# Loads of the late units in a fused attention and feed-forward kernel: start, place and planned slack

## The chip, the cores and the metric

The kernel runs on one core of one Trainium2 chip. The metric is device time in microseconds (us) of one execution; three timed runs of the kernel before stand beside one profiled execution. TensorE does the matrix products, VectorE (DVE), ScalarE (ACT) and GpSimd (POOL) the elementwise work, SyncE (SP) issues most transfers and GpSimd the others.

## The reference

Cosine attention over 8 batches, 12 heads, 448 positions and 64 columns, then a feed-forward layer with a cosine gate over all 3584 rows:

```
q_n = q / (norm(q) + 1e-6);  k_n = k / (norm(k) + 1e-6)
attn = exp(q_n @ k_n.T / tau - max);  attn = attn / (sum + 1e-9)
x = (attn @ v), heads side by side        # 3584 x 768
h = x @ w_in                              # 768 x 2048
out = (h * cos(h)) @ w_out                # 2048 x 768
```

Inputs and outputs are float32; the products are made in bfloat16.

## The kernel before

**Units and pairs.** The 96 heads are cut into 16 *units* of 6 heads (`u` from 0 to 15, two units for each batch), and each unit into 3 *pairs* of heads (`g` from 0 to 47). A pair takes four score products (`scores`, L709 and L717) with an exponential behind each (ACT, L724), and the attention products of the pair before (`attend`, `split`: L746 and L738 for most pairs). Sums of the exponentials of a unit are counted by matmuls (`counts`, L770), inverted, written to DRAM and read back spread over the partitions (`chain`: gather L907, spread L902 or L915, broadcast L917 into `RB`), and GpSimd makes the normalised `xT` (L922).

**First and second product.** When both units of a batch are done, `m1` makes the first product of that batch, `x @ w_in` (L935): 16 tiles in 8 steps of two, each step followed by a cosine on ScalarE (L964) and a multiplication on VectorE (L966) that gives `gT` of that step. The second product (`m2_fill`, `m2_quarters`: L1034, L1063) is cut into small pieces and filled in between the products of the following pairs. `points` names the pairs after which a first product comes: pair 12 for batch 1, and 21, 27, 33, 39, 45 for batches 2 to 6.

**The way of a unit's inputs.** `load` brings q and k of one pair of heads into `raw` (L582, two transfers on SP's queue); `raw` has two buffers, for even and odd units. GpSimd squares them (`square`, L622), VectorE sums (L629), ScalarE or GpSimd makes the inverse root, GpSimd scales (L660, `qks`), and a transfer on SP's queue transposes into `qkT` (L677, a ring of three). So the loads of unit u+2 can begin when the scaling of unit u is done. `load_v` brings a unit's v into `va` (L596, two issues on GpSimd's queue; three buffers).

**The planner.** All this is written down as a list of operations with what they read and write. `Program.arrange` plays the list through with a cost for each operation: TensorE's operations keep nearly their order (it may take one of the next eight), while on the other engines, SP's and GpSimd's queues included, each time one of the operations that are ready is taken, the one that is due first, due times being counted back from TensorE's. The outcome is the fixed order of each engine; on the chip semaphores hold the data's order. Three things steer it here. `behind` puts a transfer behind another one in its queue, without a wait for that one's data. `reads` adds a real dependency. `pad` (2.5 us, `LATE`, for loads of unit 2 and later) makes the planner expect a load's data later than it computes, and changes no instruction of its own.

**Where the late loads stand.** In `pair`, at the first pair of an even unit u, the loads of unit u+2 are put behind the broadcast of unit u-1 (`bcast`); at the last pair of an even unit, the loads of unit u+3 behind the same broadcast. At the first pair of each unit `load_v` of a later unit is put behind a making of `xT` ("x%d"), with exceptions in `PLAN["vloads"]`. From pair `behind0` on, if pair g-1 is normalised by the chain (not "direct"), the first attention product of pair g-1 is listed behind the first score product of pair g and a filling of the second product; before that pair it is listed ahead of both.

Of the kernel before, what the change touches and what calls it, by code (L numbers as in the profile page):

```python
# [13 lines left out]
PLAN = {  # L14
    "apart": 1,
    "ahead": (1, 2),
    "halves": tuple(range(25)),
    "folded": (0, 1, 2, 3),
    "grid": {2: (16, 5, 6), 3: (11, 3, 4), 4: (8, 2, 3)},
    "hold": 0.6,  # L20
    "margin": 1.0,
    "sq": ["AA", "A", "A", "P", "P", "P"],
# [4 lines left out]
    "late4": {1: (7, "T9"), 2: (8, "T10")},  # L27
    "power": (2,),
    "late": 0.0,
    "behind0": 13,  # L30
    "inverted": (5, 7, 9, 11, 13, 15),
    "bi": 0.0,
    "sooner": {8: 20, 12: 20},
# [20 lines left out]
    "given": {13:(0,0,2,3),16: (4, 0, 5, 2), 22:(1,2,5,6), 26:(3,2,5,6), 27:(0,0,3,2), 34: (12, 4, 5, 6), 46: (12, 4, 3, 4), 47: (4, 0, 5, 0)},  # L54
    "roots": (3, (8, 0), (10, 0), (12, 0), (14, 0)),
    "lead": {33: 5, 45: 5, 12: 13, 21: 13},
    "vloads": {3: [(4, "x6"), (5, "x6")], 4: [(6, "x11")], 5: [], 6: [(7, "x15"), (8, "x15")]},
    "behind": {2: 8, 3: 0, 4: 8},
    "direct": (0, 1, 2, 3, 4, 5, 7, 8, 9, 10, 11, 17, 23, 47),
}  # L60
# [340 lines left out]
def bass_cosine_attention__then__act_gcu_kernel(  # L401
# [30 lines left out]
    LATE = 2.5  # L432
# [22 lines left out]
    gT = sb("gT", [128, NF * RING], BF16)  # L455
# [123 lines left out]
    def load(u, p0, p1, apart=False, eng="SP", behind=None, reads=()):  # L579
        i = u % 2  # L580
        h = slice(2 * p0, 2 * p1)
        f = [lambda e, x=x, t=t: e.dma_start(  # L582
            rawv[i][BP * x : BP * x + BP, h].rearrange("p h s d -> p h (s d)"), src(t, u, 2 * p0, 2 * (p1 - p0)))
            for x, t in enumerate((k, q))]
        for x in ((0,), (1,)) if apart else ((0, 1),):
            behind = P.ops[-1] if x == (1,) else behind
            dma(eng, [f[y] for y in x], list(reads), [("raw", i, p, y) for p in range(p0, p1) for y in x] + (["first"] if (u, p0) == (0, 0) and 1 in x else []),
                "raw%d_%d_%s" % (i, p0, x), 0.97 * (p1 - p0) * len(x), "load u%d p%d" % (u, p0), behind, 1.8,
                pad=LATE if u > 1 else 0.0)

    def load_v(u, behind=None, reads=()):
        if u >= NU:
# [349 lines left out]
    def m1(b, early=0, split=NKC, turn=TURN, order=tuple(range(NKC)), done=0, inner={}):  # L942
        table(SINSET)

        def names(gi):
            return BANKS.get(PHs[turn[gi]][0], [PHs[turn[gi]][0]])

        def step(gi, a, c0, c1):
            m1_step(b, turn[gi], 2 * gi + a, c0, c1, order)

        for gi in range(done):
            for a in range(2):
                step(gi, a, NKC - 2, NKC - 1)
        for c0, c1 in [(0, split)] + [(c, c + 1) for c in range(split, NKC - 1)]:
            for gi in range(done, early):
                for a in range(2):
                    step(gi, a, c0, c1)
        for gi in range(NF // 2):
            for g in inner.get(gi, ()):
                transposes(g)  # L960
            ph, cz = PHs[turn[gi]][1], gi % 2
            for a in range(2):
                step(gi, a, NKC - 1 if gi < early else 0, NKC)
            act(lambda e, ph=ph, cz=cz: e.activation(cosv[cz], ph[:, :, 0:S], ACT.Sin, bias=cst.ap()[:, 0:1], scale=1.0),  # L964
                names(gi) + ["cst0"], [("cos", cz)], 2 * S, "S", 1, label="sin%d.%d" % (b, gi))
            dve(lambda e, ph=ph, cz=cz, gi=gi: e.tensor_tensor(  # L966
                gTv[:, 2 * gi : 2 * gi + 2, S * (b % 2) : S * (b % 2) + S], ph[:, :, 0:S], cosv[cz], ALU.mult),
                names(gi) + [("cos", cz)], [("gT", b % 2, gi)], 2 * S, label="g%d.%d" % (b, gi))
        table(EXPSET)
# [13 lines left out]
    def m2_add(b):  # L983
        for t in range((b * S) // 128, ((b + 1) * S) // 128):
            w = [0, HW, DM]
            if t == B * S // 128 - 1 and PLAN["tail"]:
                w.insert(2, HW + PLAN["tail"])
            for hf, x in enumerate(zip(w, w[1:])):
                m2_queue.append([t, hf, 0, None, x])
# [108 lines left out]
    def find(label):  # L1098
        return [o for o in P.ops if o.label == label][-1]
# [23 lines left out]
    def direct(g):  # L1123
        return g in PLAN["direct"]
# [16 lines left out]
    points = {PB * (b + 1) + (PLAN["second"] if b == 1 else 3): b for b in range(1, B - 1)}  # L1141

    def pair(g, f):
        u, p = g // UP, g % UP
        if 3 <= u < NU - 1:
            if p == 0:
                norms(u + 1, 0)
            if p == u % 2:
                norms(u + 1, 1)
        late = g > PB  # L1150
        quarters = g >= PB
        if late and not direct(g - 1):
            f = (f[0] + f[1], 0) + f[2:]
        behind = g - 1 in points or g >= PLAN["behind0"] and not direct(g - 1)
        if late and not behind and g - 1 not in PLAN["quarters"]:
            attend(g - 1, direct(g - 1), (0,))
        scores(g, 0)
        m2_fill(f[0], quarters)
        if late and behind and g - 1 not in PLAN["quarters"]:
            attend(g - 1, direct(g - 1), (0,))  # L1160
        scores(g, 1)
        if late and g - 1 in PLAN["quarters"]:
            m2_fill(f[1], quarters)
            attend(g - 1, direct(g - 1), (3, 0))
            scores(g, 2)
            attend(g - 1, direct(g - 1), (1, 2))
        elif late and direct(g - 1):
            attend(g - 1, True, (1, 2))
        elif late:
            attend(g - 1, False, (1,))  # L1170
            m2_fill(f[1], quarters)
            if not f[1]:
                scores(g, 2)
            attend(g - 1, False, (2,))
        elif 1 <= g < PB:
            if g in PLAN["ahead"] and g + 1 < PB:
                transposes(g + 1)
            attend(g - 1, direct(g - 1))
        closes = g > PB and not direct(g - 1) and (g % UP == 0 or direct(g))
        closes = closes and g not in points  # L1180
        if closes:
            if f[1]:
                scores(g, 2)
            m2_fill(f[2], quarters)
            counts((g - 1) // UP)
        if g >= 1 and g != PB:
            if closes:
                chain((g - 1) // UP)
            if g % UP == 0:
                if g > PB and (u <= 3 or u % 2 == 0):  # L1190
                    for x in range(UP if u + 2 < NU else 0):
                        load(u + 2, x, x + 1, behind=find("bcast%d" % (2 if u == 4 else u - 1)) if u > 3 else
                             find(PLAN["u5"][x]) if u == 3 else None)
                if g > PB:
                    for x, y in PLAN["vloads"].get(u, [(u + 2, "x%d" % (g - 1 if u % 2 == 0 else g - 4))]):
                        load_v(x, find(y))
        if g == PB:
            m2_fill(f[1], True)
        if g + 2 < PB:
            norms((g + 2) // UP, (g + 2) % UP)  # L1200
        if g + 1 < PB and g not in PLAN["ahead"]:
            transposes(g + 1, g + 1 < PLAN["apart"])
        if max(TD, PB + 2) <= g + 2 < NG and g + 2 >= LT:
            transposes(g + 2)
        for x, (y, t) in PLAN["late4"].items():
            if y == g:
                load(4, x, x + 1, behind=find(t))
        if PLAN["v3"] and g == PLAN["v3"][0]:
            load_v(3, None, [PLAN["v3"][1]])
        if not closes:  # L1210
            if not late or direct(g - 1) and g - 1 not in PLAN["quarters"] or not direct(g - 1) and f[1]:
                scores(g, 2)
            m2_fill(f[2], quarters)
        scores(g, 3)
        m2_fill(f[3], quarters)
        if p == UP - 1 and u >= 3 and u % 2 == 0:
            loads(u + 3, find("bcast%d" % (u - 1)) if u > 4 else None)
# [37 lines left out]
    for g in range(PB, NG):  # L1255
        pair(g, PLAN["six"] if g == PB else PLAN["given"][g] if g in PLAN["given"] else shares(PLAN["cycle"].get(g, 2)))
        if g in points:
            if 0 < m2_at() and m2_at() + 6 >= 2 * NF:
                m2_fill(2 * NF - m2_at(), True)
            if not direct(g - 1):  # L1260
                counts((g - 1) // UP)
                chain((g - 1) // UP)
            if points[g] == 1:
                m1(1, 2, *PLAN["mixed"])
            else:
                m1(points[g], 2, UP, PLAN["turns"].get(points[g], AFTER))
            m2_add(points[g])
            m = (NF - 5 - m2_at()) % NF or NF
            m2_fill(PLAN["lead"][g] if g in PLAN["lead"] else m + NF if m < 8 else m, True)
# [50 lines left out]
```

## Time and profile before

| | us |
|---|---|
| median of 3 runs | 422.16 |
| lowest, highest | 420.97, 422.93 |
| the profiled execution, its own time | 421.63 |
| its span, first to last instruction | 419.8 |
| TensorE busy | 408.0 |
| ScalarE busy | 272.6 |
| GpSimd busy | 248.3 |
| VectorE busy | 198.2 |
| mean granted TensorE clock | 0.996 of full speed |

All times of the profile are counted from the first instruction of the span. "Busy" of TensorE is the time in which at least one matmul is in the array; matmuls are pipelined, and their ends are modelled. PEld are its weight loads, which overlap. "SPq" and "POOLq" are the issues of transfers. In a row of the timeline the bracket gives the idle time before the instructions and what ended it; "issue" means that the profile shows nothing that the engine waited for. In a row of the waits the three numbers are the total in us, the number of times and the longest. A row of the stretches has the stretch, its length, busy time and instructions of PE, PEld, DVE, ACT and POOL, the granted clock, the DMA share and GB/s. DMA queue q8 carries instructions: packets, MB and share.

### The profile page before, as it was taken

How to read it: one execution, taken by the hardware profiler on the slowest of the kernel's cores; microseconds unless marked ns; L12 is line 12 of the kernel's file. 1: busy time of each engine (PE TensorE's matmuls, PEld its weight loads, DVE VectorE, ACT ScalarE, POOL GpSimd, SP SyncE). 2: the span in 40 equal slices, each digit the busy share in tenths (PEclk: the TensorE clock that was granted, in tenths of full speed). 3: DMA queues.
4: the chain of work that ended last, by engine and by line, in shares of the span. 5: the costliest groups of instructions: out<-in, count | busy, mean ns of one | idle time of the engine just before them, and what ended most of it. 6: DMA issues, size and time to landing. Idle time of an engine off the chain costs nothing.

```text
span 419.8 us, 13928 instructions
## 1 busy us (share of the span) xinstructions
PE 408.0 (97%) x6213; PEld 245.6 (59%) x6213; DVE 198.2 (47%) x277; ACT 272.6 (65%) x386; POOL 248.3 (59%) x196
## 2 busy tenths in 40 slices
PE   7899999999999999999999999997999999999997
PEld 3354556755666656664567556773567655655555
DVE  4474753446753277245833376332853344313511
ACT  5897588894989557894588547881488735714500
POOL 4999985889493796878392994639664311020000
PEclk9999999999999999999999999998999999999999
DMA  8999999989878996499838994799914920141023
GB/s 189 251 251 226 207 211 211 234 128 224 124 108 171 211 278 117 104 219 184 194 71 152 199 232 111 110 204 191 218 28 86 187 69 3 44 116 38 2 66 85
DMA packets 78736, 63.54 MB, mean 151 GB/s; under 512 B 41844, under 2 KB 72916, under 8 KB 78676
## 3 DMA queue, kind: packets, MB, share of 16 engines
q1 hardware_dynamic: 60468, 49.96, 56.2%
q0 software_dynamic: 18048, 12.59, 20.8%
q8 instruction: 49, 0.80, 0.9%
q10 hardware_dynamic: 160, 0.10, 0.1%
q14 instruction: 11, 0.09, 0.1%
HBM read 54.98 MB, written 11.19 MB: 158 GB/s over the span
## 4 chain that ended last, share of the span: by engine, by line
PE 90%; DMA 3%; ACT 3%; DVE 2%; issue 1%; POOL 0%; SPq 0%; ACTq 0%
PE MP L1034 27%; PE SC L935 20%; PE AV L935 12%; PE SC L709 6%; PE AV L746 4%; PE MP L1063 4%; PE AV L770 4%; PE SC L1063 3%; DMA va<-in_v_dram 3%; PE MP L935 2%; PE AV L819 2%; ACT PX L724 1%; PE AV L810 1%; PE AV L803 1%; PE SC L717 1%
## 5 line engine op out<-in xcount | busy, mean ns | idle before, releaser
L724 ACT ACTIVATE PX<-SC 128x448 bf16<-128x448 f32 (+1 forms) x192 | 149.1, 825 | 14.8 <-PE SC L709 8.8
L1034 PE MATMUL MP<-W,gT 64*64 64x384 bf16 x2816 | 135.6, 323 | 0.7 <-DVE qkT L698 0.6
L1034 PEld LDWEIGHTS MP<-W,gT 64*64 64x64 bf16 x2816 | 81.0, 107 | 34.8 <-issue 4.8
L660 POOL TENSOR_TENSOR qks<-raw,rn 128x896 bf16<-128x896 f32 (+1 forms) x48 | 79.6, 1678 | 21.9 <-ACT rn L652 21.5
L935 PE MATMUL SC<-xT,W 128*128 128x448 bf16 x444 | 91.5, 354 | 0.0
L622 POOL TENSOR_TENSOR sq<-raw 128x896 bf16<-128x896 f32 x44 | 73.5, 1688 | 8.5 <-DMA raw<-in_q_dram 7.3
L922 POOL TENSOR_TENSOR xT<-xu,RB 128x448 bf16<-128x448 f32 x34 | 37.8, 1137 | 55.4 <-DMA RB<-scr 55.4
L935 PEld LDWEIGHTS SC<-xT,W 128*128 128x128 bf16 x444 | 43.3, 98 | 40.7 <-issue 1.3
L964 ACT ACTIVATE cosb<-SC,cst 128x896 f32<-128x896 f32 x37 | 37.3, 1007 | 38.7 <-PE SC L935 36.8
L935 PE MATMUL AV<-xT,W 128*128 128x448 bf16 x276 | 60.9, 357 | 0.7 <-issue 0.7
L629 DVE TENSOR_REDUCE n<-sq 128x14 f32<-128x896 bf16 (+2 forms) x49 | 51.6, 1058 | 5.7 <-ACT sq L620 4.7
L966 DVE TENSOR_TENSOR gT<-SC,cosb 128x896 bf16<-128x896 f32 x37 | 40.2, 1088 | 26.8 <-ACT cosb L964 26.7
L709 PE MATMUL SC<-qkT 64*64 64x448 bf16 x576 | 52.4, 353 | 0.3
L964 ACT ACTIVATE cosb<-AV,cst 128x896 f32<-128x896 f32 x23 | 23.2, 1008 | 40.7 <-PE AV L935 39.1
L756 DVE COPY xu<-AV 128x448 f32<-128x448 f32 x34 | 21.2, 625 | 51.5 <-PE AV L738 51.5
L935 PEld LDWEIGHTS AV<-xT,W 128*128 128x128 bf16 x276 | 26.9, 99 | 26.0 <-DVE xs L781 1.1
L1001 DVE COPY osb<-MP 128x384 f32<-128x384 f32 x26 | 14.5, 557 | 47.7 <-PE MP L1034 36.6
L746 PE MATMUL AV<-PX,va 64*64 64x448 bf16 x408 | 35.6, 349 | 0.0
L966 DVE TENSOR_TENSOR gT<-AV,cosb 128x896 bf16<-128x896 f32 x23 | 25.0, 1088 | 21.3 <-ACT cosb L964 21.3
L889 POOL TENSOR_TENSOR xT<-xu,RB 128x448 bf16<-128x448 f32 x8 | 9.1, 1135 | 29.9 <-ACT RB L885 29.9
L596 POOL DMA_DIRECT2D va<-in_v_dram x32 | 22.1, 694 | 7.0 <-DMA raw<-in_q_dram 4.2
L709 PEld LDWEIGHTS SC<-qkT 64*64 64x64 bf16 x576 | 17.3, 106 | 12.4 <-ACT PX L724 5.6
(84 smaller groups left out, 390.5 us busy)
## 6 DMA issues: line engine op xcount, KB each, us to landing
raw<-in_k_dram SPq DMA_DIRECT2D x48, 224.0 KB, 5.6
raw<-in_q_dram SPq DMA_DIRECT2D x48, 224.0 KB, 6.1
out_dram<-osb SPq DMA_DIRECT2D x54, 192.0 KB, 3.5
va<-in_v_dram POOLq DMA_DIRECT2D x32, 192.0 KB, 8.3
RB<-scr SPq DMA_DIRECT2D x18, 336.0 KB, 4.5
W<-in_moe_w_in_dram POOLq DMA_DIRECT2D x4, 768.0 KB, 14.7
W<-in_moe_w_out_dram POOLq DMA_DIRECT2D x4, 768.0 KB, 19.2
RB<-scr SPq DMA_DIRECT2D x6, 224.0 KB, 3.7
```

The lines of the kernel that those rows point to most:

```text
L622: pool(lambda e, x=x, y=y: e.tensor_tensor(y, x, x, ALU.mult), src_, dst, 0.1 + n * 1.78e-3, label="sq%d.%d" % (u, p)).pad = LATE if u > 1 ...
L629: dve(lambda e, w=w: e.tensor_reduce(out=n2v[i][:, 2 * p : 2 * p + 2, w], in_=sqv[p][:, :, w, :], axis=mybir.AxisListType.X, op=ALU.add), ...
L660: f = lambda e, s0=s0, s1=s1: e.tensor_tensor(qksv[i][:, p, s0:s1].rearrange("p s h d -> p h s d"), rawv[i][:, h, s0:s1, :], bass.AP(rn[i] ...
L709: m = e.matmul(SCv[z][BP * o : BP * o + BP, a, 0:S], t[r, c - 1 + (NT3 + 1) * o, 0:BP], t[r, :, BP : 2 * BP], start=True, stop=True)
L724: act(lambda e: e.activation(PHv[j] if c == 0 else PXv[j][:, c - 1], SCv[z][:, :, 0:n], ACT.Exp, scale=1.0 / TAU), ["SC%d" % z], [("PX", j ...
L746: m = e.matmul(AVv[64 * a : 64 * a + 64, o, 0:S], vav[y][r, 2 * p + a, c + 1, :], PXv[j][r, c, a, :], start=(c == 0), stop=False)
L922: f = lambda e, p=p: e.tensor_tensor(xTv[b % 2][:, UP * i + p, :].rearrange("p (s o m) -> p o s m", s=NB, o=2), xuv[:, u % 3, p, :].rearra ...
L935: t = e.matmul(ph[:, a, 0:S], W1v[:, order[c], 128 * n : 128 * n + 128], xTv[b % 2][:, order[c], :], start=(c == 0), stop=(c == NKC - 1))
L964: act(lambda e, ph=ph, cz=cz: e.activation(cosv[cz], ph[:, :, 0:S], ACT.Sin, bias=cst.ap()[:, 0:1], scale=1.0), names(gi) + ["cst0"], [("c ...
L966: dve(lambda e, ph=ph, cz=cz, gi=gi: e.tensor_tensor(gTv[:, 2 * gi : 2 * gi + 2, S * (b % 2) : S * (b % 2) + S], ph[:, :, 0:S], cosv[cz], ...
L1034: r = e.matmul(POH[b][x : x + 64, 0:HW], gTv[k, y, col + x : col + x + 64], W2v[k, y, HW * b : HW * b + HW], start=(y == 0 and h == 0), st ...
L1063: r = e.matmul(po[:, 0 : w[1] - w[0]], gTv[:, y, col : col + 128], W2v[:, y, w[0] : w[1]], start=(y == 0), stop=(y == NF - 1))
```

## The change

The loads of units 10, 12 and 14 (issued from units 8, 10 and 12) lose their place behind a broadcast. The loads of v of units 9 to 15 leave their places behind `xT`; each is listed behind a first product and reads a step of its `gT`: unit 9 step 6 of batch 2's, and units 10 and 11, 12 and 13, 14 and 15 steps 2 and 6 of the products of batches 3, 4 and 5. The pad of loads of units 10 to 15 becomes 5.0 us. `behind0` goes from 13 to 19; as pair 12's successor is a point and pair 17 is direct, this bears on pairs 14 to 17.

```diff
-    "behind0": 13,
+    "behind0": 19,
+    "early": 8,
+    "slack": 5.0,
+    "vsteps": {2: (None, 6), 3: (2, 6), 4: (2, 6), 5: (2, 6)},
...
-    "vloads": {3: [(4, "x6"), (5, "x6")], 4: [(6, "x11")], 5: [], 6: [(7, "x15"), (8, "x15")]},
+    "vloads": {3: [(4, "x6"), (5, "x6")], 4: [(6, "x11")], 5: [], 6: [(7, "x15"), (8, "x15")], 7: [], 8: [], 9: [], 10: [], 11: [], 12: [], 13: []},
...
-                pad=LATE if u > 1 else 0.0)
+                pad=(LATE if u < 10 else PLAN["slack"]) if u > 1 else 0.0)
...
-                        load(u + 2, x, x + 1, behind=find("bcast%d" % (2 if u == 4 else u - 1)) if u > 3 else
+                        load(u + 2, x, x + 1, behind=find("bcast%d" % (2 if u == 4 else u - 1)) if 3 < u < PLAN["early"] else None if u > 3 else
                              find(PLAN["u5"][x]) if u == 3 else None)
...
+            for x, y in enumerate(PLAN["vsteps"].get(points[g], ())):
+                if y is not None:
+                    load_v(2 * points[g] + 4 + x, None, [("gT", points[g] % 2, y)])
```

## The prediction

> **What bounds the kernel now.** I read the page first, then the waits of TensorE, then busy time by stretch, then the chain of waits around the one stretch that stands out, then the queues of SyncE (SP) and GpSimd (POOL) there. The page's head and its line for the instruction queue:
>
> ```profile
> span 419.8 us, 13928 instructions
> PE 408.0 (97%) x6213; PEld 245.6 (59%) x6213; DVE 198.2 (47%) x277; ACT 272.6 (65%) x386; POOL 248.3 (59%) x196
> q8 instruction: 49, 0.80, 0.9%
> ```
>
> TensorE is busy 97% of the span. So an edit that touches no TensorE work can pay only where TensorE stands still: 419.8 - 408.0 = 11.8 us, much of it the start and the tail. Its waits:
>
> ```profile
> PE AV L770 <- issue: 2.1, 1, 2.1
> PE MP L684 <- POOL qks L660: 1.9, 2, 1.3
> PE MP L1093 <- DVE gT L1092: 1.1, 1, 1.1
> PE AV L935 <- issue: 0.7, 1, 0.7
> ```
>
> The second and third lie in the first stage, which nothing here touches. The first and fourth wait for nothing that the profile shows ("issue"). They lie here (the chain around 284 us, then the timeline of TensorE at 191 us):
>
> ```profile
> 282.74 1.17 PE AV L770 x44
> 283.90 2.15 issue
> 286.05 0.28 PE AV L770 x4
> ```
> ```profile
> 191.17 0.35 PE L935 MATMUL AV<-xT,W 128*128 128x448 bf16 x1 [0.66 <-issue]
> ```
>
> The first gap splits one run of 48 equal count matmuls after the 44th, with no semaphore between them. What can be missing there is the instruction itself. The q8 line supports it: 49 blocks, and 6213 matmuls + 6213 weight loads = 12,426 instructions, 254 per block. So TensorE's program arrives in blocks of about 254 instructions, over the engines that carry the data. Now the stretches:
>
> ```profile
> 170.00:180.00 10.00, 10.00 (x256) 6.84 (x252) 2.82 (x5) 8.79 (x16) 7.47 (x6) 1.00 0.58 123
> 180.00:190.00 10.00, 10.00 (x230) 6.40 (x222) 4.81 (x9) 8.76 (x12) 8.36 (x9) 1.00 1.24 205
> 190.00:200.00 10.00, 9.34 (x50) 4.76 (x49) 5.39 (x7) 3.93 (x4) 7.69 (x5) 1.00 1.31 198
> 260.00:270.00 10.00, 10.00 (x268) 8.14 (x264) 3.14 (x6) 8.28 (x13) 9.15 (x7) 1.00 0.72 138
> 270.00:280.00 10.00, 10.00 (x252) 7.03 (x248) 3.05 (x5) 7.80 (x11) 0.14 (x1) 1.00 0.85 149
> 280.00:290.00 10.00, 7.85 (x129) 4.33 (x122) 3.19 (x5) 3.69 (x5) 9.92 (x10) 0.86 1.20 186
> 290.00:300.00 10.00, 10.00 (x53) 5.13 (x52) 6.40 (x7) 4.36 (x5) 8.80 (x5) 0.97 0.87 222
> ```
>
> The last three columns are the granted clock, the DMA share and GB/s. Both gaps fall at DMA shares of 1.2 to 1.3. Among the small matmuls of the pairs TensorE eats 252 + 248 = 500 instructions in 10 us, a block in 5.1 us; in a first product 53 + 52 = 105, a block in 24 us. A block that comes some us late therefore hurts in the pairs or just behind them, and hardly inside a product. The 2.15 us gap also costs clock: 10 x (1 - 0.86) + 10 x (1 - 0.97) = 1.7 us. Together the place costs 2.15 + 1.7 = **3.85 us**, the other 0.66 us.
>
> SP's queue shows what is in the way. At the first place twelve load transfers stand within 14 us, at the second a broadcast, six of them and two transposes; the last row, from the page, gives a transfer's size:
>
> ```profile
> 175.96 1.31 SPq L917 DMA_DIRECT2D RB<-scr  x2
> 178.67 0.61 SPq L582 DMA_DIRECT2D raw<-in_k_dram  x1
> 185.39 0.67 SPq L582 DMA_DIRECT2D raw<-in_q_dram  x1
> 192.75 0.61 SPq L582 DMA_DIRECT2D raw<-in_q_dram  x1
> ...
> 272.68 1.31 SPq L917 DMA_DIRECT2D RB<-scr  x2
> 274.03 0.61 SPq L582 DMA_DIRECT2D raw<-in_k_dram  x1
> 278.44 0.61 SPq L582 DMA_DIRECT2D raw<-in_q_dram  x1
> 279.16 4.89 SPq L677 DMA_TRANSPOSE qkT<-qks  x2
> 287.44 0.61 SPq L582 DMA_DIRECT2D raw<-in_k_dram  x1
> ```
> ```profile
> raw<-in_k_dram SPq DMA_DIRECT2D x48, 224.0 KB, 5.6
> ```
>
> The transposes took 4.89 us to issue: SP's path was full. I estimate the backlog at 279 us: six transfers of 224 KB are 1.34 MB, at the 205 GB/s of the 180 to 190 stretch 6.5 us from 274.03, so to past 280.5, the broadcast not counted. My reading, an inference, is that the block is fetched behind this backlog.
>
> **The change part by part.** *Early q and k loads.* Only the loads of units 10, 12 and 14 lose the order behind a broadcast (3 x 6 transfers); units 11, 13 and 15 keep it. A load is now free to start once the scaling (POOL qks) of the unit two before it is done:
>
> ```profile
> 164.72 3.34 POOL L660 TENSOR_TENSOR qks<-raw,rn 128x896 bf16<-128x896 f32 x2 [3.47 <-ACT rn L652]
> 213.85 8.28 POOL L660 TENSOR_TENSOR qks<-raw,rn 128x896 bf16<-128x896 f32 x5
> 242.92 1.69 POOL L660 TENSOR_TENSOR qks<-raw,rn 128x896 bf16<-128x896 f32 x1
> 257.59 4.98 POOL L660 TENSOR_TENSOR qks<-raw,rn 128x896 bf16<-128x896 f32 x3 [6.66 <-ACT rn L652]
> ```
>
> Unit 8's last two pairs are scaled by 168.0, unit 10's by 217.2 (two of five), unit 12's first by 244.6 and its last two by 260.9 (two of three). So unit 10's loads move from 178.67 to 168 or earlier, unit 14's from 274.03 to 261 or earlier, about 11 to 13 us; they go from a stretch with share 1.24 to one with 0.58 (and from 0.85 to 0.72). Behind the broadcast then stand the loads of 11, 13 and 15, which the planner can now let follow at once. As these are due later than unit 14's were, the transposes, which are due first, can pass them. The removed pile is worth, at the second place, between 0 (unit 15 takes unit 14's slot and all stays) and 3.85 us; at the first, where six of the twelve transfers leave, and the V loads among them, between 0 and 0.66. I take 3.85 and 0.5: the gap has to shrink only below what turns the clock down, and the 0.66 us gap turned nothing down.
>
> What the earlier loads may hit: four loads (0.9 MB, 4.4 us by the rate above) now lie among pairs, at 168, 217 and 261, in front of a transpose or a code block. In the trace of before no load of a late unit lies there. A gain is excluded, since nothing stands still there now; the bounds are 0 and the dearest stop shown, 3.85 us, each. I take 0.2 each, 0.6 in all, as the six loads at 226 us of the old order stopped nothing:
>
> ```profile
> 226.26 0.61 SPq L582 DMA_DIRECT2D raw<-in_k_dram  x1
> 229.51 0.61 SPq L582 DMA_DIRECT2D raw<-in_q_dram  x1
> 230.22 2.22 SPq L677 DMA_TRANSPOSE qkT<-qks  x1
> ```
>
> *V loads.* Seven units' V loads (9 to 15) get a real wait for gT step 2 or 6 of a product. Each is two POOL issues:
>
> ```profile
> 283.13 1.34 POOL L596 DMA_DIRECT2D va<-in_v_dram  x2
> DMA to landing us min/median/max: 3.8/8.3/15.8
> ```
>
> The 1.34 us stay; the order moves. Behind the waiting issue on POOL's in-order queue stand squares and scalings. A product is 16 x 6 = 96 matmuls, at 53 in 10 us 18 us, with 8 gT steps, so an issue that stands one step too early holds them up to 2.3 us. What hides it: POOL had 0.14 us of work in 270 to 280, and what it feeds, the transposes, has the rest of the product. The last V load goes out inside the product that begins at 286, so by 304, and lands by 304 + 15.8 = 320; its first use lies behind the next product. I count 0. Without that cover it would cost up to 2.3 us for each of seven.
>
> *Planned slack, 5.0 for 2.5 us.* No instruction is added. The planner puts work on loads of units 10 to 15 up to 2.5 us later into POOL's order; POOL's free time above hides it: 0. A gain is excluded, as TensorE waits for no load; at most it costs the longest wait of TensorE for a scaling shown, 1.3 us.
>
> *behind0 19.* In pairs 14 to 17 the first attention product goes ahead of the first scores. There ScalarE is the limit beside TensorE (its busy time is the fourth after the stretch's length, PE first); the last row is a score product from the chain:
>
> ```profile
> 106.00:111.00 5.00, 4.96 (x120) 3.05 (x115) 3.33 (x4) 4.93 (x7) 3.72 (x3) 1.00 0.95 154
> 111.00:116.00 5.00, 4.94 (x116) 2.84 (x112) 4.43 (x7) 5.00 (x8) 0.00 (x0) 1.00 0.52 60
> ```
> ```profile
> 280.76 0.19 PE SC L709 x4
> ```
>
> ScalarE idles 0.07 us of 10 us. Scores that come one such product later (0.19 us of TensorE for four overlapping matmuls) cost at most 4 x 0.19 = 0.8 us; a gain is bounded by TensorE's 0.10 us of idle time in these rows. I take +0.25.
>
> Sum on the profiled execution: 421.63 - 3.85 - 0.5 + 0.6 + 0.25 = 418.1. The median of the runs lies 0.53 above that execution, so **418.7 us**.
>
> [...]
>
> **Rivals.** *The pile changes its owner.* Unit 15's loads stand behind the same broadcast at 272.68 and follow in the slot of unit 14's at 274.03; the transposes meet the same backlog, and only the first gap shrinks: 422.16 - 0.5 + 0.6 + 0.25 = 422.5. For it: the order behind the broadcast stays for odd units. Against: their due time is later. *Slower: the early loads stop TensorE in the pairs.* At 168, 217 and 261 a block lasts 5.1 us, and four loads take 4.4 us of transfer; if one block is requested behind all four, its fetch plus its landing passes 5.1 us and TensorE stops as at 283.90. With the old stop still there, one costs 3.85 more: 422.5 + 3.85 = 426.4. If the old stop goes, one new stop gives 422.5 again and two give 426.4. It decides from about 5 us of backlog at a block's request. For it: DMA shares of 0.58 and 0.72 leave room, but not inside 4 us. Against: the loads at 226. *The gaps are not the data's doing:* TensorE halts at these instructions whatever is moved, and only the costs remain: 422.16 + 0.6 + 0.25 = 423.0. For it: the gap at 191 lies inside a product, where a block lasts 24 us. Against: both lie at the highest DMA shares. *The change doesn't do what it says:* the planner puts the loads in the old places, since SP takes whichever ready transfer is due first: 422.2.
>
> **How the numbers follow.** What a measurement here can tell is about 0.5%, 2.1 us (three runs spread 420.97 to 422.93). Forecast 0.47, from 416.5 (both gaps gone, no costs: 417.6, less half the runs' spread) to 420.0 (the scores' full 0.8, another 0.75 lost to blocks). The owner changes 0.22, another cause 0.05, no move 0.04, all within 0.5% of 422.16: 0.31. New stops 0.22, slower. The range 416.5 to 424.8 leaves out most of the slower case's 0.22, and takes in the rest; the likeliest case's own range is 416.5 to 420.0. Faster 0.47, same 0.31, slower 0.22.
>
> **What would show it.** Right: no "issue" wait of over 1 us for TensorE near 284, a granted clock of 1.00 in 280 to 300, loads on SP near 168, 217 and 261, V issues on POOL only inside products. Wrong: the 2.15 us gap at the same run of matmuls (the owner changed), or "issue" gaps in the pairs at 165 to 175, 215 to 225, 258 to 270 (new stops). TensorE's busy sum should stay near 408 less 1.7. If it waits for qkT or xT at L709 or L935 instead, a term that I set at 0 was wrong.

## The result and the profile after

| | before | after |
|---|---|---|
| median of 4 runs | 422.41 us | 417.82 us |
| lowest, highest | 420.97, 422.93 | 416.91, 418.58 |
| the profiled execution, its own time | 421.63 | 417.67 |
| its span | 419.8 | 415.9 |
| TensorE busy | 408.0 | 406.4 |
| mean granted clock | 0.996 | 1.000 |

The ratio is 0.9896, with a 95% interval of 0.9864 to 0.9928: faster by 1.0%, 4.6 us in the medians. A second comparison, later and beside other kernels, gave 0.9872 (0.9827 to 0.9918). A ratio leaves out the runs that lie over 1.5% above their own kernel's fastest and a median does not, so of a kernel that scatters, as the one before does, the ratio drops the slowest runs.

The head of the page after, and its instruction queue:

```profile
span 415.9 us, 13931 instructions
PE 406.4 (98%) x6213; PEld 246.7 (59%) x6213; DVE 197.5 (47%) x277; ACT 272.4 (66%) x386; POOL 248.5 (60%) x196
q8 instruction: 49, 0.80, 0.8%
```

The work is the same: as many matmuls, as many code blocks, the same bytes. TensorE's waits after, in the same columns as before (total, times, longest):

```profile
PE MP L687 <- POOL qks L663: 2.4, 3, 1.5
...
PE AV L773 <- issue: 0.4, 1, 0.4
...
PE AV L938 <- issue: 0.2, 1, 0.2
```

Before, there were two waits for nothing: 2.15 us at 284 and 0.66 us at 191. The one near 191 is 0.15 us here, and at 284 there is none; the 0.38 us at L773 lies at 268, among the pairs, where TensorE did not wait before (three lines of the program more, so L770 is L773 now). The chain around 284, after:

```profile
281.01 1.79 PE MP L1037 x44
282.80 1.26 PE AV L773 x48
284.06 0.67 PE SC L938 x3
284.73 1.14 PE AV L938 x6
285.87 0.57 PE SC L938 x3
286.44 0.38 PE AV L938 x2
286.81 0.38 PE SC L938 x2
287.19 0.38 PE AV L938 x2
```

The 48 count matmuls run through. From their first to the end of these pieces it is 287.57 - 282.80 = 4.77 us. Before, the same pieces of the chain were

```profile
286.05 0.28 PE AV L770 x4
286.33 0.68 PE SC L935 x3
287.00 2.02 PE AV L935 x6
289.02 1.12 PE SC L935 x3
290.14 0.63 PE AV L935 x2
290.77 0.38 PE SC L935 x2
291.15 0.38 PE AV L935 x2
```

and took 291.53 - 282.74 = 8.79 us: 4.02 us more, 2.15 of it the gap and nearly all of the rest the halved clock (0.50 granted from 287.1 to 290.5), which shows in the six matmuls that took 2.02 and now take 1.14 us. The whole gain in this pair of profiles, 3.9 us of span, is the size of this one place; the other differences cancel.

SP's queue in the last pairs before that product, after:

```profile
262.19 0.69 SPq L585 DMA_DIRECT2D raw<-in_k_dram  x1
...
264.26 0.61 SPq L585 DMA_DIRECT2D raw<-in_q_dram  x1
264.97 2.45 SPq L680 DMA_TRANSPOSE qkT<-qks  x1
...
274.38 2.43 SPq L920 DMA_DIRECT2D RB<-scr  x2
276.92 1.25 SPq L680 DMA_TRANSPOSE qkT<-qks  x1
278.21 0.60 SPq L585 DMA_DIRECT2D raw<-in_k_dram  x1
...
281.81 0.61 SPq L585 DMA_DIRECT2D raw<-in_q_dram  x1
```

Unit 14's last four transfers have moved to 262 to 264. Unit 15's six now follow the broadcast in the place that unit 14's had, but a transpose passes them and they begin at 278.21 instead of 274.03. Two stretches after:

```profile
260.00:270.00 10.00, 9.62 (x248) 7.50 (x240) 3.05 (x5) 7.26 (x11) 9.77 (x7) 1.00 1.24 195
280.00:290.00 10.00, 10.00 (x150) 6.55 (x141) 2.79 (x5) 5.38 (x7) 8.31 (x6) 1.00 1.23 224
```

The granted clock is 1.00 in 280 to 290, yet the DMA share there is 1.23, as high as before (1.20). So the share of a stretch does not tell whether TensorE stops. And 260 to 270, once 0.72, is now 1.24 and has 20 matmuls fewer.

### The profile page after: what moved, and what is told of

Same layout as the page of the kernel before. It is cut to its first block, busy times and chain, and to the rows that moved or that the text cites. A ratio compares the mean times of both kernels' runs of the same rounds, so it can differ in the third digit from the quotient of the medians.

```text
span 415.9 us, 13931 instructions
## 1 busy us (share of the span) xinstructions
PE 406.4 (98%) x6213; PEld 246.7 (59%) x6213; DVE 197.5 (47%) x277; ACT 272.4 (66%) x386; POOL 248.5 (60%) x196
## 4 chain that ended last, share of the span: by engine, by line
PE 92%; POOL 3%; DVE 2%; ACT 1%; DMA 1%; issue 1%; SPq 0%; ACTq 0%; POOLq 0%
PE MP L1037 28%; PE SC L938 20%; PE AV L938 12%; PE SC L712 6%; PE AV L749 5%; PE MP L1066 4%; PE AV L773 4%; PE SC L1066 3%; PE MP L938 2%; PE AV L822 2%; POOL qks L663 1%; PE SC L720 1%; PE AV L813 1%; PE MP L837 1%; PE AV L1066 1%; DMA raw<-in_q_dram 1%
## 5 line engine op out<-in xcount | busy, mean ns | idle before, releaser
L1037 PE MATMUL MP<-W,gT 64*64 64x384 bf16 x2816 | 136.1, 323 | 0.7 <-DVE qkT L701 0.6
L1037 PEld LDWEIGHTS MP<-W,gT 64*64 64x64 bf16 x2816 | 81.8, 107 | 33.5 <-issue 4.8
L938 PE MATMUL AV<-xT,W 128*128 128x448 bf16 x276 | 59.7, 352 | 0.2 <-issue 0.2
L599 POOL DMA_DIRECT2D va<-in_v_dram x32 | 22.0, 693 | 23.2 <-DVE gT L969 18.6
```

Of the source, the lines that this page charges most:

```text
L938: t = e.matmul(ph[:, a, 0:S], W1v[:, order[c], 128 * n : 128 * n + 128], xTv[b % 2][:, order[c], :], start=(c == 0), stop=(c == NKC - 1))
L1037: r = e.matmul(POH[b][x : x + 64, 0:HW], gTv[k, y, col + x : col + x + 64], W2v[k, y, HW * b : HW * b + HW], start=(y == 0 and h == 0), st ...
```

## The experiments

Twelve kernels ran, in three groups of four, in the order of the table. All times are medians; the ratio is to runs of the kernel before, beside them on the same chip. The kernel before scattered widely there (416.97 to 426.50 with a median of 421.69 in the first group, 420.25 to 427.18 with 422.48 in the second, 418.19 to 429.26 with 422.50 in the third), so I read each kernel by its ratio, by its median against that of the kernel before, and by the gaps of its one profile. In the edits, values of `PLAN` are written out and "..." stands for code left out.

| kernel | us | ratio | 95% interval |
|---|---|---|---|
| before + loads only | 419.86 | 0.9998 | 0.9968 to 1.0028 |
| before + V only | 419.65 | 0.9956 | 0.9909 to 1.0003 |
| before + slack only | 423.19 | 1.0043 | 1.0001 to 1.0084 |
| before + order of attention only | 422.37 | 1.0056 | 1.0007 to 1.0106 |
| whole change, again | 417.47 | 0.9872 | 0.9827 to 0.9918 |
| change without V | 420.41 | 0.9963 | 0.9927 to 0.9998 |
| change without loads | 419.44 | 0.9944 | 0.9912 to 0.9975 |
| change without order of attention | 418.11 | 0.9915 | 0.9880 to 0.9950 |
| before + 152 instructions | 423.15 | 1.0026 | 0.9986 to 1.0065 |
| after + 152 instructions | 419.44 | 0.9961 | 0.9931 to 0.9992 |
| before, unit 14's transfers small | 419.81 | 0.9945 | 0.9905 to 0.9986 |
| before + V of unit 9 only | 422.72 | 1.0045 | 1.0001 to 1.0089 |

### Each part alone

**Loads only.**

```diff
-    load(u + 2, x, x + 1, behind=find("bcast%d" % (2 if u == 4 else u - 1)) if u > 3 else
+    load(u + 2, x, x + 1, behind=find("bcast%d" % (2 if u == 4 else u - 1)) if 3 < u < 8 else None if u > 3 else
```

> The kernel before with one part of the change: the loads of units 10, 12 and 14 lose their place behind the broadcast. Pile theory (TensorE's 2.15 us gap at 284 us is a late block of its own instructions, fetched behind the transfers that SP has queued): the gap at 284 goes, granted clock 1.00 there, the gap at 191 shrinks below 0.3 us, and some tenths are lost in the pairs at 258 to 275 to the loads that now lie there; 418.5 to 419.5 us. V theory (the V issues on GpSimd's queue near both gaps are what fills the engines): both gaps stay, 422.4. Slack theory (the order by due times that the slack of 5.0 us gives is what counts): the gap stays, about 422.

No gap for nothing was left at 191 or 284, as the pile theory has it. But the profile has a wait that I had not named:

```profile
PE MP L1037 <- DVE gT L969: 2.5, 2, 1.5
```

VectorE's timeline at that place shows where it comes from:

```profile
162.68 0.33 DVE L917 RECIPROCAL rcp<-sums 128x28 f32<-128x28 f32 x1 [4.07 <-DMA sums<-xs]
162.92 1.03 DVE L969 TENSOR_TENSOR gT<-AV,cosb 128x896 bf16<-128x896 f32 x1
...
164.86 1.08 DVE L969 TENSOR_TENSOR gT<-SC,cosb 128x896 bf16<-128x896 f32 x1
```

The gather of unit 6's sums is a transfer of 14 KB, issued at 152.23 us, but VectorE waits 4.07 us for it, the last two multiplications of the product stand behind that in its order, and TensorE's second product waits for them. So a pile of transfers has a second victim: not code, but the small transfer behind it. What this part alone is worth is not settled: by the ratio, 0.9998, nothing; by the medians, 419.86 against 421.69, 1.8 us, where my pile theory gave 2 to 3 us.

**V only.**

```diff
-    "vloads": {..., 6: [(7, "x15"), (8, "x15")]},
+    "vloads": {..., 6: [(7, "x15"), (8, "x15")], 7: [], 8: [], 9: [], 10: [], 11: [], 12: [], 13: []},
+    "vsteps": {2: (None, 6), 3: (2, 6), 4: (2, 6), 5: (2, 6)},
...
+            for x, y in enumerate(PLAN["vsteps"].get(points[g], ())):
+                if y is not None:
+                    load_v(2 * points[g] + 4 + x, None, [("gT", points[g] % 2, y)])
```

> The kernel before with only the V loads of units 9 to 15 moved into first products. SP's order is then the same as before. Pile theory: the gap at 284 stays whole, since the V load there was issued at 283.13, as the gap began at 283.90; the one at 191, with V issues at 182.68 and 188.48 ahead of it, may shrink from 0.66 to 0 to 0.3: 421.8 to 422.4 us. V theory: both gaps go, 418 us. GpSimd shows waits of up to 2 us for gT, and TensorE none.

The gap at 284 was there, but smaller, and that at 191 gone:

```profile
PE AV L773 <- issue: 1.3, 2, 1.0
```

The longer of the two is the one at 284; the other lies at 234. The interval of the ratio, 0.9909 to 1.0003, just takes in no change, and the medians differ by 2.0 us. Neither expectation is met: the V moves seem to do more than nothing, and less than all.

**Slack only.**

```diff
-                pad=LATE if u > 1 else 0.0)
+                pad=(LATE if u < 10 else 5.0) if u > 1 else 0.0)
```

> The kernel before with only the planned slack of the loads of units 10 to 15 at 5.0 us. In SP's order two pairs of unit 15's loads now follow unit 14's after one transpose. Pile theory: the pile before 284 is larger, the gap stays at 2 us or grows, 422 to 424 us. Slack theory: the gap goes, 418 to 419 us.

The gap was there, behind a longer pile, but with 1.5 us and no lower clock (1.00 from 280 to 300 us) it did not grow. The median of 423.19 lies in the pile theory's range, and the slack theory's 418 to 419 us is out; but this profile also has a wait for gT of 2.2 us, so the pile at 284 is not shown to have set the time.

**Order of attention only.**

```diff
-    "behind0": 13,
+    "behind0": 19,
```

> The kernel before with only the order of the first attention product changed in pairs 14 to 17. SP's and GpSimd's orders are the same as before. My prediction's step: +0.25 us (0 to 0.8) between 106 and 125 us, both gaps as before, 422.4 to 422.9 us. Rival: ScalarE, the limit there, gets its scores sooner for a better packing, -0.1 to -0.5 us. Either lies within the noise of the runs; the profile's times at the end of pair 17 tell.

The stretch itself hardly varies. From the first matmuls of batch 1's product to the counts that close pair 17, two rows of TensorE's timeline before, and two of this kernel:

```profile
86.55 1.31 PE L935 MATMUL MP<-xT,W 128*128 128x448 bf16 x6
...
123.82 0.95 PE L770 MATMUL AV<-PX,mark 128*32 128x224 bf16 x32
```
```profile
86.43 1.31 PE L935 MATMUL MP<-xT,W 128*128 128x448 bf16 x6
...
123.64 0.95 PE L770 MATMUL AV<-PX,mark 128*32 128x224 bf16 x32
```

That is 37.27 against 37.21 us, and the change without this part has 37.27 again where the change has 37.22: the order is worth 0.05 us. The ratio of 1.0056 is then not its doing: SP's and GpSimd's orders are those of before, and this profile shows a gap of 2.36 us that ends at 195, with the clock down to 0.83 in that stretch, and the wait for gT of 2.5 us; at 284, where the same transfers are queued as before, it has no gap at all. What differs between two runs of one transfer order is chance, and it is worth several us.

```profile
190.00:200.00 10.00, 7.64 (x67) 3.74 (x56) 2.76 (x4) 2.92 (x4) 9.50 (x8) 0.83 1.55 128
```

### The whole change and each part undone

> The whole change once more, beside the kernels that undo a part of it. Two mechanisms are on trial. Code theory: TensorE's instruction blocks come late behind SP's pile (gaps at 191 and 284). Gather theory, new from the single parts: the small gather of unit 6's sums lands late behind the loads and the V load of unit 9 at 146, VectorE waits for it in order with its reciprocal, and TensorE then waits 2 to 2.5 us for gT near 163. Both: ratio to before 0.986 to 0.993, no issue gap over 0.6 us, no wait for gT at L1037 in the profile. Rival (the first comparison was luck of a kernel whose runs scatter): 0.997 to 1.003.

0.9872 repeats the gain. Its one profile, an execution of 421.17 us where the median is 417.47, misses the expectation of no gap over 0.6 us and shows what the change does not rule out:

```profile
267.79 1.16 PE AV L773 x42
268.95 1.75 issue
270.70 0.37 PE AV L773 x6
...
285.93 1.32 issue
```

The same two gaps, in a bad run: 1.75 us where the first profile had 0.38, 1.32 where it had none. There is no wait for gT at L1037.

**Without V.**

```diff
-    "vsteps": {2: (None, 6), 3: (2, 6), 4: (2, 6), 5: (2, 6)},
+    "vsteps": {},
-    "vloads": {..., 6: [(7, "x15"), (8, "x15")], 7: [], 8: [], 9: [], 10: [], 11: [], 12: [], 13: []},
+    "vloads": {..., 6: [(7, "x15"), (8, "x15")]},
```

> The changed kernel with the V loads back in their old places. Gather theory: unit 9's V load is back at 146, VectorE's reciprocal waits 3 to 4 us for the sums, TensorE waits 2 to 2.5 us for gT near 163; 1.5 to 2.5 us slower than the whole change. Code theory alone: at most 0.5 us slower, by the gap at 191. Rival (V moves are worth nothing): the same time as the whole change.

2.9 us slower than the whole change in the medians, 0.0091 in the ratios, and the intervals (0.9827 to 0.9918, 0.9927 to 0.9998) do not meet. The profile shows not the wait that the gather theory named, but a third victim at batch 4's product, the broadcast whose data GpSimd needs for xT, and the gap at 285:

```profile
PE AV L938 <- POOL xT L925: 1.5, 3, 1.2
PE AV L773 <- issue: 1.3, 1, 1.3
```

That victim is not one of V's bytes: no V load goes out between 199 and 240 us in this profile. Undoing the V moves also changed SP's order. The first two loads of unit 14 and a transpose now stand ahead of the broadcast of unit 9, which the changed kernel issues before them, at 226.70:

```profile
225.97 0.61 SPq L585 DMA_DIRECT2D raw<-in_k_dram  x1
...
228.56 2.11 SPq L680 DMA_TRANSPOSE qkT<-qks  x1
230.72 1.30 SPq L920 DMA_DIRECT2D RB<-scr  x2
```

So the 2.9 us are the price of undoing the V moves with all that the planner reorders for it; how much of them is V's bytes is not shown.

**Without the early loads.**

```diff
-    "early": 8,
+    "early": 99,
```

> The changed kernel with the loads of units 10, 12 and 14 back behind the broadcast. Code theory: the pile at 274 to 285 is back and with unit 15's loads even longer, the issue gap near 284 is back with 1.5 to 2.2 us and its clock with 1.7: 2 to 4 us slower than the whole change. Rival (the V moves do it all): the same time as the whole change.

2.0 us slower in the medians, 0.0072 in the ratios (the intervals 0.9912 to 0.9975 and 0.9827 to 0.9918 just overlap), with the gap back at its place, without a lower clock (1.000 over the whole profile):

```profile
PE AV L773 <- issue: 1.7, 1, 1.7
```

**Without the order of attention.**

```diff
-    "behind0": 19,
+    "behind0": 13,
```

> The changed kernel with the old order of the first attention product in pairs 14 to 17. SP's and GpSimd's orders are those of the changed kernel. My prediction's step: 0.25 us faster than the whole change (0 to 0.8). Rival: 0.1 to 0.5 us slower, since ScalarE is fed better in the new order. The noise of the runs is larger than either; the profile's times from 105 to 125 us decide.

418.11 us, 0.9915: not to be told from the whole change.

### The mechanism itself

**152 instructions more, and no transfer moved.**

```diff
-    P.filler = (lambda e, shut: e.matmul(PO[:, 0:S], zt[:, 0:128], zt, start=shut, stop=shut), zero, MM, 0.3)
+    P.filler = (lambda e, shut: [e.matmul(PO[:, a:b], zt[:, 0:128], zt[:, a:b], start=shut, stop=shut)
+                                 for a, b in ((0, 149), (149, 298), (298, 448))][-1], zero, MM, 0.3)
```

> The kernel before, with each of the 38 idle-time matmuls of the first stage cut into three that together cover the same columns: 152 instructions more on TensorE at the start, and nothing else; all other engines' orders are those of before. Each block boundary then falls 152 instructions (some 3 us in the pairs) earlier in the program. Code theory: the boundary of 279 us goes to about 276 and the next to 281, whose instructions are needed only inside the slow product; the one of 184 goes to 181 and 186. Both gaps go, with no transfer moved: 417.5 to 420 us (0.988 to 0.996), unless a boundary falls badly elsewhere (231 to 236 us is the likeliest, up to 1 us). Rivals (TensorE halts for data, or at the same instructions): both gaps stay at their instructions, 422.

> The changed kernel with the same 152 instructions at the start. Code theory: the small gaps of its runs at 268 and 284 (0.3 to 1.8 us, by chance of the run) go, since no boundary is then needed in the last pair before the product: 415 to 417.5 us and a smaller scatter, unless boundaries fall badly elsewhere. Rival: the same gaps at the same instructions, 417.5.

The place was right and the time was not. In the kernel before, the gaps left the 48 counts at 284 and the product at 191 (no wait for nothing at L770 or L935 is left) and longer ones came up at other instructions:

```profile
PE MP L1034 <- issue: 3.7, 3, 2.3
```
```profile
74.21 0.33 PE L1034 MATMUL MP<-W,gT 64*64 64x384 bf16 x4
76.86 0.52 PE L1034 MATMUL MP<-W,gT 64*64 64x384 bf16 x8 [2.33 <-issue]
```

One of 2.33 us and one of 0.66 us in the pairs of batch 1, and one of 0.75 us a little ahead of the counts near 286, inside the run of second-product matmuls. Data and semaphores of those matmuls are as before; only where the block boundaries fall has changed. That speaks against both rivals, data and fixed instructions.

The instruction queue's own packets settle what the gaps wait for. Before the gap of 2.15 us ended at 286.05, a block of 16 KB (q8 has 0.80 MB in 49) had come in on q8 from 283.44 to 284.60; before the one of 2.33 us ended at 76.86, one had come in from 74.27 to 75.25. It is so throughout: the fourteen profiles have 24 waits of TensorE for nothing of over 0.25 us between 64 and 400 us, and each ends 1.2 to 1.7 us after a block has landed. TensorE was waiting for that code. When a block was asked for, the profile does not show; that it came late because of the data in its way rests on the tests here.

The test also shows that the boundaries' places decide which pile stops TensorE: here the two at 70 to 83 fell badly, which I had not looked at, and the time did not improve (1.0026). The changed kernel with the same instructions scattered little (418.81 to 421.64), but its 419.44 us miss the 415 to 417.5 expected and its ratio, 0.9961, is above the 0.9872 of the change, so it is no better version.

**Small transfers of unit 14.**

```diff
-        return bass.AP(t.tensor, ..., [..., [S * D, nh], [1, NB * D]])
+        return bass.AP(t.tensor, ..., [..., [S * D, nh], [1, D if u == 14 else NB * D]])
...
-            rawv[i][...].rearrange("p h s d -> p h (s d)"), src(t, u, 2 * p0, 2 * (p1 - p0)))
+            rawv[i][...].rearrange("p h s d -> p h (s d)")[:, :, 0 : D if u == 14 else NB * D], src(...))
```

> The kernel before, where the q and k transfers of unit 14 bring one of their seven blocks of rows: six sevenths of unit 14's q and k are left out. All orders stay. Code theory: the pile at 274 to 283 us is 1.15 MB smaller, the gap near 284 goes, the one at 191 stays: 418.5 to 420.5 us. Rivals (a fixed instruction, or V): the gap at 284 stays, 422.

The chain at the place, with the bytes gone and every order kept:

```profile
285.95 1.79 PE MP L1034 x44
287.74 1.26 PE AV L770 x48
289.00 0.67 PE SC L935 x3
```

No gap, as expected if it hangs on the bytes of those six transfers. This one profile alone does not decide it, since the kernel with the order of attention only had none there either, with all the bytes; but the time fell too, to 419.81 us with a ratio of 0.9945 (0.9905 to 0.9986), although the gap at 191 stayed, with 2.64 us.

**V of unit 9 alone.**

```diff
-    "vloads": {..., 6: [(7, "x15"), (8, "x15")]},
+    "vloads": {..., 6: [(7, "x15"), (8, "x15")], 7: []},
+    "vsteps": {2: (None, 6)},   # and the loop that reads it
```

> The kernel before with the V load of unit 9 alone moved into the product of batch 2 (146 to about 161 us). Gather theory: what the V moves bring beside the late gaps is that unit 6's sums land sooner; no wait of TensorE for gT near 163 in the profile, 1 to 2 us faster than before in the mean of runs (about 420.5 to 421.5, since the gap of 2.5 us showed in three of five profiles with this load at 146), the gap at 284 as before. Rival (it is the later V loads that count): 422, as before.

The wait for gT near 163 did not show, as in no other of the seven profiles with this load at 161; with it at 146, five of seven have it, of 0.9 to 2.5 us. But the time is no better than before (1.0045, and 422.72 us against 422.50), where 420.5 to 421.5 was expected: three gaps for nothing of 1.5, 1.3 and 1.2 us, at 183, 192 and 286, are in that profile. That the V move of unit 9 takes this wait away is borne out by 0 of 7 profiles against 5 of 7; that it pays by itself is not.

## Why the prediction was right, and where it was not

The forecast was 418.7 us, the result 417.82.

- **The bound** was read rightly: TensorE's work is untouched, and the time went where it stood still. That the missing thing is code was an inference and is now shown: each gap ends just after a block has landed, and more instructions, with no data moved, move the gaps. That the code is late because of queued data is borne out by the small transfers of unit 14, which move no instruction and bring the time down.
- **3.85 us at 284.** Measured 4.02 us by the pieces of the chain. I had bounded it from 0 to 3.85 and taken all of it because transposes might pass unit 15's loads: SP's rows after show that. What I did not see is that this is a chance, not a switch. Of the six profiles with unit 14's loads behind the broadcast, whole in size and with the block boundaries of before, the gap at the last counts is 2.15, 1.0, 1.5, 0, 1.7 and 1.2 us; of five with them early it is 0, 0, 1.3, 1.3 and 0.5. On average the gap shrinks from 1.3 to 0.6 us, so that this pair of profiles shows the whole 4 us is luck in part. The 1.7 us of clock in the term is a chance too: of the 88 runs of the kernel before in the three groups, 43 have a mean granted clock of 0.996 or less, as its profile has, and of the 12 runs of the whole change one.
- **0.5 us at 191.** Measured 0.66 - 0.15 = 0.51 in the first pair. I had named six q and k transfers and the V loads among them. Of the profiles that keep the block boundaries, five with the loads early, V moved or not, have 0 to 0.5 us near 191; two with these V loads moved and the loads late have 0 and 0.2; five with neither have 0, 0.66, 1.3, 2.36 and 2.64 us. So either move seems to be enough there.
- **0.6 us for the early loads in the pairs.** Mis-sized. From the first matmuls behind batch 4's product to the last counts (282.74 before, 282.80 after) the chain took 28.65 us before and 29.84 after, from these two rows, of before and of after:

```profile
254.09 0.94 PE MP L1034 x20
```
```profile
252.96 0.94 PE MP L1037 x20
```

That stretch, where unit 14's early loads lie, costs 1.19 us more, 0.38 of it the gap at 268, and in the second profile of the change that gap was 1.75 us. The loads of units 10 and 12 cost nothing: from the end of batch 2's first product to the start of batch 3's it is 26.90 us before and 26.89 after, from batch 3's to batch 4's 28.34 in both. This is the slower rival, on a small scale: the stop does move into the pairs.
- **0 for the V loads.** This term was wrong, in size and in sign. Undoing them costs 2.9 us in the medians, more than undoing the early loads. I had priced the issue on GpSimd, and neither the bytes, 384 KB for each unit, nor the new order that SP's queue gets from the move. For the bytes speaks the wait for gT near 163, which is gone wherever unit 9's load has moved; for the order, the broadcast at batch 4's product. What each is worth is not shown. The bound on the new wait was too low as well: GpSimd waited for gT 18.6 us in 5 waits, the longest 7.4 instead of 2.3, and nothing came of it, as the cover named there (free time, users far ahead) held.

```profile
POOL va L599 <- DVE gT L969: 18.6, 5, 7.4
```

- **0 for the slack.** Alone it was 1.0043 (1.0001 to 1.0084), and 1.5 us slower in the medians, at or past the slow end of 0 to 1.3 us, with two pairs of unit 15's loads joined to the pile. What it does within the whole change was not tried.
- **0.25 us for the order of attention.** Measured 0.05 us the other way.
- **The rivals.** "The pile changes its owner" is half true: unit 15's loads do follow the same broadcast, and in the second profile of the change the gap is there, smaller and without its clock. "Another cause" fell by the landing of the blocks and by the two mechanism tests.

The median agreed partly by cancellation: early loads cost 0.6 us more than I took, TensorE came to batch 1's product at 85.99 instead of 86.55 us, before any part of the change bears on it, and the V moves paid where I had written the gain down to the loads. So the mechanism was right, and the agreement to 0.9 us is partly luck.

## What to carry to other kernels

A wait for nothing on the engine that sets the time, in the middle of equal instructions, can be its own code standing behind queued data: look whether a block of the instruction queue lands just before the engine goes on (1.2 to 1.7 us here), then shift the code by a hundred or two instructions (152 here) where the engine idles, and see whether the gap moves. A transfer costs not only its own waiters: ask at each moment what small thing (code, a gather, a broadcast) is requested behind it and how soon that is needed, and try bulk loads where the program runs through its code slowly (here 105 instructions in 10 us of a first product, 500 in the pairs). Where a gap is a chance, one profile gives its size and not its price; undo the parts one at a time beside the whole, since each part alone may show nothing.

## What the runs showed of the hardware

Two things I had not expected. The lateness is a chance from run to run: one kernel's runs on one chip lay between 420.25 and 427.18 us, and parts that leave every transfer in its order gave gaps of 0.66 or 2.36 us in the same product. And the clock: the gaps of 2.15, 2.36 and 2.64 us brought the granted clock to half for 3.4 us each (0.50 from 287.1 to 290.5 us in the kernel before; 0.83 over 190 to 200 us with the order of attention only; a mean of 0.996 over 420.8 us with small transfers of unit 14). At those of 1.75 us (1.00 from 260 to 280 us in the second profile of the change), 1.7 us (1.000 over the whole profile without the early loads) and 1.5 us (1.00 from 280 to 300 us with the slack only; what makes the mean of that profile 0.996 lies elsewhere) it stayed up, but so it did at this one of 2.33 us (in the kernel before with 152 instructions more; the stretch that holds the gap has a clock of 1.00):

```profile
70.00:80.00 10.00, 7.67 (x187) 4.97 (x179) 2.63 (x4) 7.10 (x13) 9.45 (x7) 1.00 1.17 225
```

So the price of a gap of about 2 us was here its length (2.33 us) or nearly twice that (2.15 us and 1.7 us of clock); which of the two it will be, no run here tells beforehand.
